# One-core mLSTM and feed-forward kernel: w_out's scale tile moved to the state products' bank, the first product's terms regrouped, the queues reordered

## Chip, cores and metric

One Trainium2 chip, one core. The metric is the device time of one execution in microseconds, as the median of several runs.

## What is computed

An mLSTM layer over B = 4, H = 8, S = 768, D = 40, written below as a loop over time, and behind it a feed-forward layer whose middle is h times softmax(h), normalised by rows. The output is 3072 x 320.

```python
m_new = maximum(f + m, i)
C = exp(f + m - m_new) * C + exp(i - m_new) * outer(v, k)
n = exp(f + m - m_new) * n + exp(i - m_new) * k
y = sigmoid(o) * (C @ q) / maximum(abs(n @ q), 1)
...
h = x @ w_in                                  # 320 -> 1024
solu = h * softmax(h)
ln = (solu - mean) / sqrt(var + 1e-6) * g_ln
out = ln @ w_out                              # 1024 -> 320
```

## The kernel before

The time loop is cut into six chunks of 128 steps. A unit is one chunk of one batch; there are 24 units, `u = 4 * c + b`, four for each chunk `c`, and units of one batch hand on the state `C`. What a unit does, in order of its data:

- Gates and scores. ScalarE (ACT) makes a 128 x 1024 decay tile `d` by exponentials (L1225 for the first four units, from a matmul spread L1158; L1214 for the others, from `gb`, which is loaded and masked by GpSimd (POOL, L1199)). TensorE (PE) makes scores (L1283, two banks of PSUM), VectorE (DVE) multiplies them with `d` to `p` (L1296).
- `y`. TensorE multiplies `q` with the state (L1323, units from 4 on) and `p` with `v` (L1350, two halves) into a third bank, VectorE scales and divides (L1336, L1365 to L1377), GpSimd multiplies with the sigmoid of the output gate (`x`, L1391; the sigmoids of eight units are taken at once, L1252). TensorE makes the state's increment (L1419).
- First product. `x` becomes two f16 tiles, a high and a low part (`xq`, ACT L1456 and POOL L1463, L1470), turned by a DMA transpose (L1484) to `xT`. TensorE multiplies `xT` with `w_in`, held as high (`wih`) and low (`wil`) f16 parts, into `ph`, 1024 columns: two half-depth matmuls (L1500) and then seven terms of two matmuls of 512 columns each (L1514), which are queued as three operations of two, two and three terms.
- Middle and second product. DVE and ACT make `us` from `ph` (L1530 to L1596), a DMA transpose turns it (`big<-us`, L1605), TensorE multiplies it with `w_out`'s high and low parts in four operations of six matmuls of 320 columns (L1660), ACT scales it to `ot` (L1677), which is stored.

The weights come as pairs of 32-bit words and are decoded, scaled and split on the chip in the first third of the run. For `w_in`: ACT L790 and DVE L800, L809 decode, ACT L858 sums magnitudes, the largest goes through TensorE (L880, L893) and DVE makes the scale `wsc` (L904); then ACT scales (L932) and casts the high part (L942, L955), POOL subtracts for the low part (L939), and small DMAs lay the last rows (L967). For `w_out`: L790, L800, L809, ACT L1005 sums, DVE L1023 to L1025 takes the largest and that of `g_ln` (`g`, L1684), TensorE transposes (L1028), DVE reduces (L1032), TensorE spreads (L1039), DVE makes `gs` and `ow` (L1046 to L1050), then ACT and DVE make the high and low parts (L1057, L1067).

The work of all units and of the set-up is a list of 1,314 numbered operations with reads and writes. Their order on every queue is a table, `ORDER`; each engine works its queue strictly in that order. A pair `(a, b)` in the table is a joint operation: the matmuls of two operations of TensorE are issued interleaved. A triple `(a, -1, n)` puts `n` filler matmuls (L1698, on the identity, results unused) ahead of operation `a`; operations in `BESIDE` get a small unused matmul after each step (L1702). Tiles are rings: a tile's first writer waits until the last user of the tile that had the buffer is done. Rings that matter here: `ph` has two PSUM tiles, `sy` three banks (scores, `y`), `so_` one bank (state increments and second products). `P.place` sets a tile's place in its ring's order; the small tile in which w_out's scale is made (`WOR`) stands in `ph` ahead of unit 0's product (place -0.4).

```python
for n in range(filled.get(n, 0)) ...          # fillers, in run()
steps = [((i + 0.5) / f.n, i, f) for f in (a, b) for i in range(f.n)]
for _, i, f in sorted(steps, key=lambda t: t[:2]):
    f.step(self, i)                           # a joint operation
```

Of the kernel before, what the change touches and what calls it, by code (L numbers as in the profile page):

```python
# [39 lines left out]
def gdv(P):  # L40
# [5 lines left out]
BESIDE = (235,)  # L46
WIR, WOR = ("sy", -0.5), ("ph", -0.4)
# [424 lines left out]
def mlstm_moe_kernel(ctx: ExitStack, tc: tile.TileContext, tok, qkT, og, fi0, fg, ig, w_in, w_out, gln, out):  # L472
# [646 lines left out]
    def unit(u):  # L1119
# [371 lines left out]
        ph = ("ph", u)  # L1491
# [4 lines left out]
        w_2 = [(*WIH, 4), (*WIL, 4), (*WIL, 5)]  # L1496
# [259 lines left out]
```

## Time and profile before

| what | us |
|---|---|
| median of 3 runs (283.72 to 286.01) | 283.91 |
| profiled execution: its own time | 283.8 |
| profiled execution: span, first to last instruction | 282.0 |
| PE busy in the span | 272.2 |
| ACT busy | 219.3 |
| DVE busy | 198.0 |
| POOL busy | 168.7 |

PE's busy time is that of its matmul records; where a matmul is issued while the one before still drains, the records overlap, so what TensorE is paid for an operation is read from the starts of successive rows and not from the durations. PEld are the loads of stationary operands, which overlap. DMA share is the mean busy share of the 16 DMA engines. All DMAs are issued from one queue (SP). Line numbers are those of the kernel before; in the changed kernel the same statements stand one or two lines lower.

### The profile page before, as it was taken

What the parts mean: (1) busy time and instruction counts of PE and PEld (TensorE: products, weight loads), DVE (VectorE), ACT (ScalarE), POOL (GpSimd) and SP (SyncE); (2) the same over time, 40 slices, a digit from 0 to 9 for tenths busy, and PEclk for the clock granted to TensorE, in tenths of its full rate; (3) what the DMA queues carried; (4) which work ended last, traced back from release to release, by engine and by line L of the source; (5) the groups of instructions that cost most, each with busy time, mean ns of one, the idle gap of its engine ahead of it and who ended that gap; (6) DMA issues with size and microseconds to landing.
All of it is one profiled execution on the core that took longest, in us unless ns stands there. A gap on an engine that the chain in (4) does not pass through costs nothing.

```text
span 282.0 us, 6383 instructions
## 1 busy us (share of the span) xinstructions
PE 272.2 (97%) x2253; PEld 214.1 (76%) x2253; DVE 198.0 (70%) x460; ACT 219.3 (78%) x473; POOL 168.7 (60%) x278
## 2 busy tenths in 40 slices
PE   6999999999997999999999999999999999999994
PEld 6977997877885787788787787888777886755673
DVE  3948885999977396776777968475887656656740
ACT  3778999999979778877749888898767749556851
POOL 5015999865864787584458764793757932653410
PEclk9999999999999999999999999999999999999999
DMA  6999989899999896799999999969799992457511
GB/s 210 369 397 364 283 184 256 236 219 246 264 304 218 220 235 149 167 226 247 166 275 217 301 198 313 196 152 197 244 213 263 217 236 54 92 108 160 88 50 46
DMA packets 85440, 60.49 MB, mean 215 GB/s; under 512 B 68016, under 2 KB 75312, under 8 KB 85408
## 3 DMA queue, kind: packets, MB, share of 16 engines
q1 hardware_dynamic: 85408, 60.08, 87.6%
q8 instruction: 18, 0.29, 0.4%
q14 instruction: 14, 0.11, 0.2%
HBM read 39.16 MB, written 4.26 MB: 154 GB/s over the span
## 4 chain that ended last, share of the span: by engine, by line
PE 75%; DMA 9%; POOL 4%; DVE 4%; issue 4%; ACT 2%; SPq 0%; POOLq 0%; ACTq 0%; DVEq 0%
PE ph L1514 19%; PE sy L1350 9%; PE sy L1283 6%; PE ph L1698 5%; DMA xT<-xq 5%; DMA big<-us 4%; PE sy L1323 4%; PE ph L1500 2%; PE so__1285 L1660 1%; PE so__2951 L1660 1%; PE so__3737 L1660 1%; PE ph L1158 1%; PE so__3793 L1660 1%; DVE nm L1530 1%; PE so__3093 L1660 1%
## 5 line engine op out<-in xcount | busy, mean ns | idle before, releaser
L1660 PEld LDWEIGHTS <-big 128*128 128x128 f16 x576 | 61.8, 113 | 20.1 <-DMA big<-us 2.7
L1350 PEld LDWEIGHTS sy<-tk,p 128*128 128x128 f32 x384 | 57.9, 192 | 4.7
L1514 PE MATMUL ph<-wih,xT 128*128 128x512 f16 x192 | 60.7, 381 | 0.0
L1350 PE MATMUL sy<-tk,p 128*128 128x41 f32 x384 | 55.6, 246 | 0.0
L1214 ACT ACTIVATE d<-gb,bG 128x128 f32<-128x128 f32 x160 | 50.6, 391 | 5.5 <-POOL kt L1265 2.8
L1514 PEld LDWEIGHTS <-xT 128*128 128x128 f16 x336 | 37.8, 118 | 17.8 <-issue 1.4
L1514 PE MATMUL ph<-wil,xT 128*128 128x512 f16 x144 | 48.8, 381 | 0.0
L1296 DVE TENSOR_TENSOR p<-sy,d 128x512 f32<-128x512 f32 x48 | 32.4, 683 | 8.6 <-PE sy L1283 8.1
L1589 ACT ACTIVATE us<-e,mu 128x1024 f16<-128x1024 f32 x24 | 27.3, 1143 | 9.8 <-DVE mu L1581 7.1
L1544 ACT ACTIVATE e<-ph,nh,hs 128x1024 f32<-128x1024 f32 x24 | 28.7, 1196 | 7.6 <-DVE nh L1537 5.4
L1596 DVE SCALAR_TENSOR_TENSOR us<-e,mu,us 128x1024 f16<-128x1024 f32 x24 | 31.7, 1320 | 2.8 <-ACT us L1589 2.6
L1530 DVE TENSOR_REDUCE nm<-ph 128x1 f32<-128x1024 f32 x24 | 29.2, 1217 | 5.9 <-PE ph L1514 5.8
L1553 DVE SCALAR_TENSOR_TENSOR e<-ph,e 128x1024 f32<-128x1024 f32 x24 | 29.2, 1215 | 5.9 <-ACT e L1544 5.8
L1643 POOL TENSOR_TENSOR pw<-ab,mhalf 128x1 f32<-128x1 f32 x24 | 16.6, 694 | 27.6 <-DVE ab L1637 21.6
L1199 POOL TENSOR_SCALAR_AFFINE_SELECT gb<-gb 128x1024 f32<-128x1024 f32 x20 | 23.4, 1170 | 12.0 <-DMA gb<-gd 12.0
L1323 PEld LDWEIGHTS sy<-C,qk 128*128 128x128 f32 x160 | 27.7, 190 | 3.4 <-PE sy L1283 0.5
L1463 POOL TENSOR_TENSOR xs<-x,xr 128x320 f32<-128x320 f32 x24 | 20.4, 850 | 15.9 <-DVE xr L1404 12.7
L1563 ACT ACTIVATE sq<-e,a 128x1024 bf16<-128x1024 f32 x24 | 27.4, 1140 | 0.8 <-DVE e L1553 0.7
L1391 POOL TENSOR_TENSOR x<-x,sg 128x320 f32<-128x320 f32 x24 | 21.9, 914 | 10.0 <-DVE x L1377 9.4
L1323 PE MATMUL sy<-C,qk 128*128 128x82 f32 x160 | 27.1, 257 | 0.4 <-DVE x L1377 0.4
L1283 PE MATMUL sy<-qk 64*128 64x128 f32 x384 | 26.6, 276 | 0.1
L1283 PEld LDWEIGHTS sy<-qk 64*128 64x128 f32 x384 | 24.9, 188 | 2.1 <-issue 1.1
(255 smaller groups left out, 565.4 us busy)
## 6 DMA issues: line engine op xcount, KB each, us to landing
gb<-gd SPq DMA_DIRECT2D x20, 512.0 KB, 5.2
qk<-in_qkT_dram SPq DMA_DIRECT2D x21, 448.0 KB, 5.3
tk<-in_tok_dram SPq DMA_DIRECT2D x24, 324.0 KB, 5.4
sg<-in_og_dram SPq DMA_DIRECT2D x12, 320.0 KB, 5.4
out_dram<-ot SPq DMA_DIRECT2D x24, 160.0 KB, 3.4
big<-in_w_in_dram SPq DMA_DIRECT2D x5, 512.0 KB, 6.6
big<-in_w_out_dram SPq DMA_DIRECT2D x4, 640.0 KB, 8.6
qk<-in_qkT_dram SPq DMA_DIRECT2D x3, 512.0 KB, 8.9
```

What stands on the lines that cost most here:

```text
L1214: nc.scalar.activation(out=P[d_t][:, j, n, :], in_=P[gb][:, h, :], func=AF.Exp, bias=P[BG][:, 0, c - 1, b * H + h : b * H + h + 1],)
L1283: nc.tensor.matmul(P[ps[j]][:, n * L : (n + 1) * L], lhsT=P[qk][r, 1, n, :], rhs=P[qk][r, 0, n, :], start=True, stop=True,)
L1296: lambda P, j=j: V.tensor_tensor(out=P[p_t][:, j], in0=P[ps[j]].rearrange("p (n l) -> p n l", l=L), in1=P[d_t][:, j], op=ALU.mult,),
L1323: nc.tensor.matmul(P[yk][:, n * 2 * E1 : (n + 1) * 2 * E1], lhsT=P[qk][:, 0, n, :], rhs=P[old][:, n, :], start=first_of_bank(), stop=False ...
L1350: nc.tensor.matmul(yv(P)[:, h, :], lhsT=P[p_t][:, j, n, :], rhs=v1(P)[:, h, :], start=first_of_bank(), stop=True, skip_group_check=True,)
L1514: nc.tensor.matmul(P[ph][:, j * 512 : (j + 1) * 512], lhsT=P[xT][:, a, :], rhs=P[w][:, k, j * 512 : (j + 1) * 512], start=False, stop=n == 6,)
L1530: lambda P: V.tensor_reduce(out=P[nm], in_=P[ph], axis=AX.X, op=ALU.max, negate=True),
L1544: lambda P: nc.scalar.activation(out=P[e], in_=P[ph], func=AF.Exp, bias=P[nh], scale=P[hs], accum_out=P[z]),
L1553: lambda P: V.scalar_tensor_tensor(out=P[e], in0=P[ph], scalar=2.0**-15, in1=P[e], op0=ALU.mult, op1=ALU.mult, accum_out=P[a]),
L1563: lambda P: nc.scalar.activation(out=P[sq], in_=P[e], func=AF.Square, bias=P[a], scale=-float(DFF), accum_out=P[su]),
L1596: lambda P: V.scalar_tensor_tensor(out=P[us][:, 1], in0=P[e], scalar=P[mu], in1=P[us][:, 0], op0=ALU.add, op1=ALU.subtract),
L1660: nc.tensor.matmul(P[po][:, 0:DM], lhsT=uTv(P, a)[:, k, :], rhs=P[w][:, k, :], start=n == 0, stop=n == 23)
```

## The change

Four edits: two constants (`BESIDE` and `WOR`), the order of the terms with the weights each operation waits for, and the whole table `ORDER`, of which the first lines are shown.

```diff
-BESIDE = (235,)
-WIR, WOR = ("sy", -0.5), ("ph", -0.4)
+BESIDE = (142, 281,)
+WIR, WOR = ("sy", -0.5), ("so_", 3.35)
...
 ORDER = [
-    18, 196, 19, 5, 37, 35, 3, 0, 17, 33, 34, 4, 1, 42, 289, 32, 47, 7, 127, 6, 31, 130, 8, 11, 52, 9, 10, 57, 12, 14,
...
+    0, 5, 33, 31, 18, 4, 19, 17, 37, 34, 3, 42, 1, 7, 47, 32, 127, 8, 11, 9, 52, 6, 150, 57, 243, 10, 289, 12, 20, 14,
...
-        terms = [(0, WIH, 0), (0, WIL, 0), (1, WIH, 1), (1, WIL, 1), (3, WIH, 0), (4, WIH, 1), (2, WIL, 2)]
-        w_k = [[(*w, 2 * k + j) for w in (WIH, WIL) for j in range(2)] for k in range(2)]
-        w_2 = [(*WIH, 4), (*WIL, 4), (*WIL, 5)]
+        terms = [(0, WIH, 0), (3, WIH, 0), (1, WIH, 1), (4, WIH, 1), (0, WIL, 0), (1, WIL, 1), (2, WIL, 2)]
+        w_h = [[(*WIH, 2 * k + j) for j in range(2)] for k in range(2)]
+        w_2 = [(*WIH, 4), (*WIL, 4)]
+        w_l = [(*WIL, n) for n in (0, 1, 2, 3, 5)]
...
-        for n0, n1, ws in ((0, 2, w_k[0]), (2, 4, w_k[1]), (4, 7, w_2)):
+        for n0, n1, ws in ((0, 2, w_h[0]), (2, 4, w_h[1]), (4, 7, w_l)):
```

In numbers over the whole table: fillers 65 before and 61 now (43 of them ahead of the gates' transposes L710 before, 36 now), joint operations 69 before and 63 now. From the first product on, 19 of 19 products with the state (L1323) were joint; now 15 of 20 are.

ACT's queue of the kernel before, from the scaling of w_in (`e<-e,wsc`) to the sigmoids (`sg`); `wt` decodes, `wih` is the cast of a high part, `wj,wm` a sum of w_out, `d<-ph` a decay tile:

```order
L942 CAST wih_342<-e_141 128x512
L932 ACTIVATE e_247<-e_247,wsc_333 128x512
L1225 ACTIVATE d_360<-ph_327 128x1024
L955 CAST w4_369<-e_247 128x512
L790 ACTIVATE wt_372<-big_175 128x640
L942 CAST wih_342<-e_170 128x512
L932 ACTIVATE e_170<-e_170,wsc_333 128x512
L1005 ACTIVATE wj_404,wm_403<-wg_274 128x640
L1225 ACTIVATE d_418<-ph_328 128x1024
L942 CAST wih_342<-e_170 128x512
L1252 ACT_TABLE_LOAD
L1252 ACTIVATE sg_117<-sg_117 128x2560
```

The same queue now:

```order
L791 ACTIVATE wt_332<-big_216 128x640
L956 CAST w4_335<-e_252 128x512
L933 ACTIVATE e_221<-e_221,wsc_303 128x512
L943 CAST wih_349<-e_141 128x512
L933 ACTIVATE e_221<-e_221,wsc_303 128x512
L943 CAST wih_349<-e_141 128x512
L1226 ACTIVATE d_380<-ph_314 128x1024
L943 CAST wih_349<-e_221 128x512
L791 ACTIVATE wt_397<-big_227 128x640
L1226 ACTIVATE d_408<-ph_320 128x1024
L1253 ACT_TABLE_LOAD
L1253 ACTIVATE sg_152<-sg_152 128x2560
```

One more scaling and one more decode of w_out (`wt_332`) stand ahead of the sigmoids, a sum of w_out (L1005) behind them, and what follows the sigmoids at once is now unit 0's L1401.

TensorE's queue of the kernel before, from unit 4's scores to the first product of unit 0 (`wmx` and `w` are w_out's scale):

```order
L1283 MATMUL sy<-qk_168 128x128 x8
L1323 MATMUL sy<-C_318,qk_168 128x82 x4
L1028 MATMUL ph<-ident,wmx 1x128
L1698 MATMUL ph<-ident 128x128 x2
L1039 MATMUL ph<-w_600,ones 128x1
L1500 LDWEIGHTS xT
L1500 MATMUL ph<-wih,xT 128x512
```

The same place now, and, behind the four matmuls of 512 columns shared with L1324 and four more, the place of w_out's scale:

```order
L1420 MATMUL so__544<-tk,kt_101 104x82 x4
L1284 MATMUL sy<-qk_239 128x128 x8
L1502 LDWEIGHTS xT
L1502 MATMUL ph<-wih,xT 128x512
L1502 LDWEIGHTS xT
L1502 MATMUL ph<-wil,xT 128x512
L1516 LDWEIGHTS xT
L1516 MATMUL ph<-wih,xT 128x512
L1324 MATMUL sy<-C_117,qk_239 128x82
```

```order
L1516 MATMUL ph<-wih,xT 128x512
L1516 LDWEIGHTS xT
L1516 MATMUL ph<-wih,xT 128x512
L1029 MATMUL so__616<-ident,wmx 1x128
L1516 LDWEIGHTS xT
L1516 MATMUL ph<-wil,xT 128x512
```

The product with the state moved from ahead of the first product into it, w_out's transpose from ahead of it to between its high and its low terms, and its tile from `ph` to `so_`.

SP's queue of the kernel before, from unit 4's `gb` to the first transpose (`g` is g_ln, `w4` w_in's last rows):

```order
L1172 DMA gb_367<-gd_180 128x1x1024
L1684 DMA g_389<-in_g_ln_dram 128x8x1
L1148 DMA qk1_168<-in_qkT_dram 112x1024
L967 DMA wih_342<-w4_369 64x512 x2
L967 DMA wil_407<-w4_369 64x512 x2
L1172 DMA gb_425<-gd_180 128x1x1024
L967 DMA wil_407<-w4_369 64x512 x2
L1484 DMA_TRANSPOSE xT_542<-xq_511 128x6x128
```

The same place now:

```order
L1149 DMA qk1_239<-in_qkT_dram 112x1024
L1173 DMA gb_479<-gd_361 128x1x1024
L968 DMA wih_349<-w4_335 64x512 x2
L968 DMA wil_382<-w4_335 64x512 x2
L1485 DMA_TRANSPOSE xT_518<-xq_494 128x6x128
L1686 DMA g_528<-in_g_ln_dram 128x8x1
L1145 DMA tk_533<-in_tok_dram 128x648
```

The load of `g`, six places ahead of the first transpose before, stands right behind it.

## Rows read from the trace of the kernel before

**Rows 1.** Busy time by stretch: length, PE, PEld, DVE, ACT, POOL, clock, DMA share, GB/s.

```profile
10.00:40.00 30.00, 29.85 (x276) 25.99 (x275) 22.81 (x55) 25.49 (x47) 15.93 (x20) 1.00 1.04 337
50.00:70.00 20.00, 19.63 (x159) 15.38 (x156) 19.63 (x44) 19.40 (x50) 13.57 (x20) 1.00 0.90 227
```

**Rows 2.** Waits of PE: total us, times, longest.

```profile
PE so__1285 L1660 <- DMA big<-us: 1.6, 1, 1.6
PE ph L1500 <- DMA xT<-xq: 0.8, 2, 0.6
```

**Rows 3.** Timeline of PE: start, us, operation, count, idle before and its releaser.

```profile
2.73 12.38 PE L1698 MATMUL ph<-ident 128*128 128x128 f32 x86 [2.73 <-POOL ident masks.py:199]
15.04 1.04 PE L710 MATMUL so__229<-ident,us 32*128 32x32 f32 x14
42.21 1.12 PE L1323 MATMUL sy<-C,qk 128*128 128x82 f32 x8
43.16 0.27 PE L1028 MATMUL ph<-ident,wmx 128*1 128x128 f32 x1
43.98 0.38 PE L1039 MATMUL ph<-w,ones 1*128 1x1 f32 x2
44.29 0.39 PE L1500 MATMUL ph<-wih,xT 64*128 64x512 f16 x1
```

**Rows 4.** Timeline of ACT.

```profile
16.18 0.29 ACT L722 COPY bG<-so__229 128x160 f32<-128x160 f32 x1 [1.80 <-PE so__229 L710]
23.49 1.34 ACT L932 ACTIVATE e<-e,wsc 128x512 f32<-128x512 f32 x2 [1.11 <-DVE wsc L904]
31.40 1.28 ACT L1252 ACT_TABLE_LOAD   x1
32.70 2.34 ACT L1252 ACTIVATE sg<-sg 128x2560 f32<-128x2560 f32 x1
```

**Rows 5.** Timeline of DVE, the gates' two long scans.

```profile
6.51 1.75 DVE L654 TENSOR_TENSOR_SCAN us<-p,us 32x768 f32<-32x768 f32 x1 [1.01 <-DMA p<-in_fg_dram]
10.91 1.47 DVE L678 TENSOR_TENSOR_SCAN us<-d,p 32x640 f32<-32x640 f32 x1
```

**Rows 6.** Groups of ACT by line and form, 0 to 60 us: busy, mean ns.

```profile
L932 ACT ACTIVATE e<-e,wsc 128x512 f32<-128x512 f32 x5 | 3.5, 721 | 1.1 <-DVE wsc L904 1.1
L790 ACT ACTIVATE wt<-big 128x640 f32<-128x640 f32 x4 | 3.2, 800 | 0.0
L1005 ACT ACTIVATE wj<-wg 128x640 bf16<-128x640 f32 x4 | 2.9, 730 | 0.0
```

**Rows 7.** Timeline of POOL.

```profile
35.11 1.69 POOL L1391 TENSOR_TENSOR x<-x,sg 128x320 f32<-128x320 f32 x2 [0.60 <-ACT sg L1252]
38.25 1.15 POOL L1470 TENSOR_TENSOR xq<-xs,xq 128x256 f16<-128x256 f32 x2
41.09 2.27 POOL L939 TENSOR_TENSOR wil<-e,wih 128x512 f16<-128x512 f32 x2
```

**Rows 8.** Timeline of SP, whose queue issues all DMAs.

```profile
39.42 1.31 SPq L1484 DMA_TRANSPOSE xT<-xq  x1
```

**Rows 9.** DMA issues, 25 to 43 us: count, KB each, median us to landing.

```profile
g<-in_g_ln_dram SPq DMA_DIRECT2D x1, 4.0 KB, 11.2
xT<-xq SPq DMA_TRANSPOSE x1, 3.0
```

**Rows 10.** Timeline of PE, first product of unit 3.

```profile
64.54 0.39 PE L1514 MATMUL ph<-wih,xT 128*128 128x512 f16 x1
66.14 0.59 PE L1514 MATMUL ph<-wih,xT 128*128 128x512 f16 x2
67.01 1.03 PE L1514 MATMUL ph<-wih,xT 128*128 128x512 f16 x4
```

**Rows 11.** Timeline of PE, its two longest waits behind 45 us.

```profile
57.94 0.42 PE L1323 MATMUL sy<-C,qk 128*128 128x82 f32 x2 [0.37 <-DVE x L1377]
...
90.48 0.31 PE L1660 MATMUL so__1285<-woh,big 128*128 128x320 f16 x1 [1.63 <-DMA big<-us]
```

123 rows, old and new, of the table ORDER are left out of this document.

## Prediction

> **What bounds the kernel now.** I read the waits of TensorE first, then the timelines of the queues in the first third, and last the busy time by stretch.
>
> The list of waits [rows 2] says that TensorE hardly ever waits: 1.6 us for one transpose of `us`, 0.8 for two transposes of `xT`, and a few tenths for others, one of them the 0.37 us at 57.94 [rows 11]. From the moment the first product starts, at 44.29 [rows 3], the run is thus a queue of TensorE's work with some 3 us of waits in it. What ends the run is when this queue starts, what stands in it, and those waits.
>
> Ahead of 44.29 TensorE looks just as busy [rows 1], but part of it is padding: 65 fillers stand there, 43 of them in the row of 12.38 us at 2.73 [rows 3]. What the first product waits for is read backwards. It is issued behind w_out's scale (L1039, 43.98) [rows 3]. Its input, unit 0's `xT`, was issued at 39.42 [rows 8] and landed 3.0 us later [rows 9], at 42.4. That waited for POOL's `xq` (38.25 + 1.15 = 39.40) [rows 7], a chain that begins with POOL's `x` at 35.11, which had waited for ACT's sigmoids [rows 7]. These ran from 32.70 to 35.04, behind a table load at 31.40 [rows 4]. ACT then had a full queue back to 23.49, where it had waited 1.11 us for w_in's scale, and before that 1.80 us for the gates' transposes [rows 4]. So the start of the first product is set by ACT's queue, and that by how early the gates and w_in's scale come. The DMA engines are full beside it (share 1.04 from 10 to 40 us) [rows 1], but the sigmoids' input is no longer late: its loads are moved ahead of the gates' stores.
>
> **The change part by part.**
>
> *Start of the first product.* Now the gates' first load and the load of `f` go out ahead of w_in's first block. DVE's first long scan waited 1.01 us for `f` and began at 6.51 [rows 5]; without that wait, and with the gates' small steps some 0.4 us earlier because their load is the first one issued, I put it at 5.1. The second scan ended at 10.91 + 1.47 = 12.38 [rows 5]; two decode steps that stood between them go behind, so about 9.9. The identity is POOL's first work now, so the fillers start at about 1.5 in place of 2.73; 36 of them take 36/43 x 12.38 = 10.4 us [rows 3], to about 12.0. The gates' transposes start there and not at 15.04, and are done 1.04 us later [rows 3], at 13.1. ACT's wait for them, which ended at 16.18 [rows 4], ends 3 us earlier; behind it stand w_in's decodes and sums, of which one had to follow the wait and three now do, so that about half of the 3 us is left at their end, 1.7. From there to the scale DVE and TensorE have less in between (the scale's last step is put ahead of the first `p`), which I count as 1.6 more. w_in's scale is then there at about 20.0, and ACT, which has two decay tiles to do first, begins its scalings at 20.2, not 23.49.
>
> From that row to the table load ACT needed 31.40 - 23.49 = 7.91 us [rows 4]. One scaling (0.72) and one decode (0.80) come in, one sum (0.73 and its read-out, about 0.9) goes out [rows 6]: +0.6. So the table load comes at 20.2 + 7.91 + 0.6 = 28.7 and the sigmoids end at 28.7 + (35.04 - 31.40) = 32.3, 2.7 earlier. From the start of `x` to the end of `xq` POOL took 39.40 - 35.11 = 4.3 us [rows 7]; with one low part (2.27 / 2 = 1.1) [rows 7] in between where another unit's `x` (1.69 / 2 = 0.85) and a product for `kt` stood, 3.8. The transpose is issued at 36.1 and lands at 39.1.
>
> TensorE itself gives nearly the same moment: from 15.04 to 42.21 [rows 3] it worked 27.2 us, in which 20 fillers stood; now 25 do, at 12.38/43 = 0.29 us at most +1.4, and waits of up to 1 us may go. 12.0 + 27.2 + 1.4 less those is 39.6 to 40.6. I take 40.1, that is 4.2 us early. The ends: 39.1, if TensorE does not hold it, and 42.2, if half of the lead is lost to the full DMA queue.
>
> That the first product can start there needs the regrouping: its last low weights came from POOL at 41.09 + 2.27 = 43.36 [rows 7]. The five high operations need none of the first four low blocks, and the low ones are due only some 3 us later. With the old grouping this start would be held to when POOL is through, 41 to 42.
>
> *Work that moved behind the start.* The product with unit 4's state (L1323) is now in the first product. Four terms with such a product took 66.14 - 64.54 = 1.60 us for two terms, two terms alone 67.01 - 66.14 = 0.87 [rows 10], so it costs 0.73 in company. w_out's scale costs 44.29 - 43.98 = 0.31 at its second matmul [rows 3], and a tenth at its first. Together +1.1.
>
> *Joint operations lost.* Five of the 20 products with the state now stand alone. Alone one takes 43.16 - 42.21 = 0.95 to the next operation's start [rows 3]; against 0.73 that is 5 x 0.22 = +1.1. One product with `v` and one state increment more stand alone: between nothing and as much each as those, +0.4 together.
>
> *Regrouped terms, the `beside` matmuls, w_out's tile in `so_`.* The 14 matmuls of a first product are the same, each with its own stationary load, so no cost. Four small matmuls more stand beside unit 0's `y`, in a stretch that has fillers anyway: between nothing and 0.3, taken as nothing. In `so_` the tile keeps the bank from unit 3's increment to unit 4's, and nothing is queued for that bank meanwhile; nothing.
>
> *Waits.* The wait at 90.48 (1.63) [rows 11] ends with a transpose of unit 2's `us`. In DVE's queue the last step of that `us` now stands ahead of two more steps of units 3 and 4 behind which it stood, so I take this wait as gone, and the 0.37 at 57.94 too, since unit 5's `x` has more room there: -2.0. Two thirds of the table are new, and unit 0's own `us` is made later than before (behind unit 1's exponentials and a `p`), with its second product due 3 us sooner. I take +1.2 for new waits; the bounds are nothing and 3.0, as much as the kernel before has in all.
>
> Sum: -4.2 + 1.1 + 1.1 + 0.4 - 2.0 + 1.2 = -2.4. The profiled execution took 283.8 us, 0.1 under the median shown, so 281.4 either way.
>
> **A rule against the change.** The load of `g` (L1684) now stands right behind the first transpose, and w_out's scale needs it, and TensorE has that scale between the high and the low terms of its first product. The row says 11.2 us from issue to landing for its 4 KB; a transpose in the same stretch took 3.0 [rows 9]. So most of the 11.2 is, I think, what was queued ahead of it: it went out behind w_out's last block, a `tk` and a `gb`. The Trainium skill ("DMA: Bandwidth & Descriptors", Rules for kernel authors) says that a strided last dimension is lowered to one descriptor per element, which would be 1,024 for `g`. By that page's table (Measured) an estimate at 10.5 ns a packet on 16 engines is 0.7 us, which changes nothing; the row, taken as it stands, makes the third rival.
>
> **Rivals.**
> - *Larger gain.* The lead holds and the new order has no waits to speak of: -4.2 + 2.6 - 3.0 = -4.6, 279.2. For it: TensorE waits so little already [rows 2]. Against: 300 operations of TensorE moved.
> - *The lead is given back.* From 50 to 70 us DVE is busy 19.63 and ACT 19.40 of 20 us [rows 1]. If these two set the pace there, starting TensorE early only makes it wait for `p` and `us` until 70, and the 1.5 us of lost pairs is paid as well: 283.8 + 1.5 - 1.6 (the wait at 90.48 still goes) = 283.7. Against: their early work starts earlier too.
> - *Slower: the scale of w_out stops TensorE.* `g` is issued at about 37.5. If it lands 11.2 later [rows 9], at 48.7, DVE's bound and TensorE's transpose follow at 49.3, in place of 42.8, and DVE, which works in order, holds unit 4's `y` behind it: 281.4 + 6.5 = 287.9. It costs from a landing at 42.2 on and makes the kernel slower than before from 44.7, that is 7.2 us after issue. For it: the row. Against: most of what was queued ahead of `g` then has landed by 39.
>
> **How the numbers follow.** The forecast case, 281.4 give or take 1.5, gets 0.52, nearly half of it below 281.1, which is 1% under the median (about what a measurement of this kernel can tell from no change). The larger gain gets 0.20, the lead given back 0.15, the slower case and other mishaps 0.13. So faster by over 1%: 0.25 + 0.20 = 0.45; within 1%: 0.27 + 0.15 = 0.42; slower: 0.13. The range goes from 278.3, a little under the larger gain, to 285.0, over the lead given back, and leaves out most of the slower case.
>
> **What would show it.** Right: the sigmoids end near 32.3, the first product starts near 40, `g` lands before 42, the first product's low terms follow its high ones without a gap at w_out's transpose (L1029 in the changed file), unit 2's second product starts without a wait, and TensorE's waits sum to 3 us or less. Wrong: a first product behind 42; a gap of TensorE at w_out's transpose; second products that wait for `big<-us` from unit 0 on; or single waits of TensorE on DVE spread over the last two thirds.

## The result and the profile after

The changed kernel took 280.19 us in the median of six runs (279.57 to 281.99), the kernel before 284.18 beside it (283.72 to 288.21): a ratio of 0.9864 with a 95% interval of 0.9817 to 0.9912. Timed a second time (`after_again` below) it came to 281.43 against 284.13, 0.9883 (0.9841 to 0.9925). The forecast was 281.4. The profiled execution took 281.67, with a span of 279.9; it is one of the longer ones, which matters further down. Medians are over all runs of a kernel; ratios leave out the runs more than 1.5% above its fastest, which show a lower granted clock.

Busy times of the page, to be held against the table of before: PE 0.8 us less, ACT 1.0 and POOL 2.8 less, DVE 1.7 more.

```profile
PE 271.4 (97%) x2249; PEld 213.0 (76%) x2249; DVE 199.7 (71%) x460; ACT 218.3 (78%) x473; POOL 165.9 (59%) x278
```

The set-up, which answers to [rows 3 to 8]. Timelines of DVE (the two long scans), ACT, POOL and SP:

```profile
5.07 1.74 DVE L655 TENSOR_TENSOR_SCAN us<-p,us 32x768 f32<-32x768 f32 x1
8.76 1.48 DVE L679 TENSOR_TENSOR_SCAN us<-d,p 32x640 f32<-32x640 f32 x1
```

```profile
12.67 0.30 ACT L717 ACTIVATE bG<-so__194 128x160 f32<-128x160 f32 x1 [0.53 <-PE so__194 L711]
19.56 1.95 ACT L933 ACTIVATE e<-e,wsc 128x512 f32<-128x512 f32 x3
29.25 1.28 ACT L1253 ACT_TABLE_LOAD   x1 [0.88 <-DMA sg<-in_og_dram]
30.54 2.34 ACT L1253 ACTIVATE sg<-sg 128x2560 f32<-128x2560 f32 x1
```

```profile
32.96 0.86 POOL L1392 TENSOR_TENSOR x<-x,sg 128x320 f32<-128x320 f32 x1 [1.66 <-ACT sg L1253]
35.70 0.94 POOL L1471 TENSOR_TENSOR xq<-xs,xq 128x256 f16<-128x256 f32 x2
41.79 1.16 POOL L940 TENSOR_TENSOR wil<-e,wih 128x512 f16<-128x512 f32 x1
```

```profile
36.66 1.33 SPq L1485 DMA_TRANSPOSE xT<-xq  x1
```

Each step is earlier than before by about what the forecast said: scalings 19.56 (23.49 before), table load 29.25 (31.40), transpose issued 36.66 (39.42). The transpose and `g`, DMA issues from 25 to 43 us (KB each, median us to landing), for [rows 9]:

```profile
xT<-xq SPq DMA_TRANSPOSE x1, 3.8
g<-in_g_ln_dram SPq DMA_DIRECT2D x1, 4.0 KB, 2.9
```

TensorE's timeline (first fillers, the gates' transposes, the first product, w_out's transpose, and every wait behind 45 us over 0.3 us), for [rows 3, 11]:

```profile
1.41 10.18 PE L1700 MATMUL ph<-ident 128*128 128x128 f32 x72 [1.41 <-POOL ident masks.py:199]
11.52 1.12 PE L711 MATMUL so__194<-ident,us 32*128 32x32 f32 x15
...
40.51 0.39 PE L1502 MATMUL ph<-wih,xT 64*128 64x512 f16 x1
...
43.30 0.27 PE L1029 MATMUL so__616<-ident,wmx 128*1 128x128 f32 x1
...
47.57 1.16 PE L1284 MATMUL sy<-qk 64*128 64x128 f32 x16 [0.57 <-DMA qk<-in_qkT_dram]
...
57.44 1.09 PE L1324 MATMUL sy<-C,qk 128*128 128x82 f32 x8 [0.79 <-DVE x L1378]
...
74.00 0.39 PE L1502 MATMUL ph<-wih,xT 64*128 64x512 f16 x1 [0.53 <-DVE rd L1369]
...
91.09 0.31 PE L1662 MATMUL so__1291<-woh,big 128*128 128x320 f16 x1 [1.37 <-DMA big<-us]
```

The first product starts at 40.51 and not at 44.29, 3.8 us early, right behind the landing of its `xT` (36.66 + 3.8 = 40.46). But TensorE now waits where it did not, and the wait for unit 2's `us` is still there (91.09, 90.48 before). Its list of waits, for [rows 2]:

```profile
PE so__1291 L1662 <- DMA big<-us: 1.4, 1, 1.4
PE sy L1324 <- DVE x L1378: 0.8, 1, 0.8
PE sy L1284 <- DMA qk<-in_qkT_dram: 0.6, 1, 0.6
PE ph L1502 <- DVE rd L1369: 0.5, 1, 0.5
```

and the two stretches of [rows 1]; from 50 to 70 us PE does less than before (19.21 busy, 19.63 before):

```profile
10.00:40.00 30.00, 29.82 (x279) 25.52 (x279) 24.05 (x59) 26.18 (x50) 17.06 (x19) 1.00 1.02 326
50.00:70.00 20.00, 19.21 (x160) 14.77 (x160) 18.22 (x39) 18.91 (x46) 14.41 (x23) 1.00 0.95 244
```

To see where the time is won, the two runs are compared at places by which TensorE has done exactly the same operations in both (fillers and the small matmuls of `BESIDE` aside, which all stand ahead of them): the starts of the first product (its half-depth matmul) of units 3, 5, 6 and 14. In us, read from the timelines of TensorE; the last column is the end of the last matmul, and the first (unit 0) shows the start only, since less work stands ahead of it now. The kernels below "changed" are the experiments, in which the same holds.

| kernel | unit 0 | unit 3 | unit 5 | unit 6 | unit 14 | last end |
|---|---|---|---|---|---|---|
| before | 44.29 | 63.33 | 83.03 | 95.08 | 170.51 | 278.46 |
| changed | 40.51 | 62.68 | 83.28 | 95.06 | 170.41 | 276.41 |
| after_again | 41.16 | 62.69 | 83.16 | 95.04 | 170.39 | 276.37 |
| hold_start | 42.15 | 62.88 | 82.95 | 94.61 | 169.96 | 276.17 |
| old_terms | 40.24 | 61.77 | 81.78 | 93.31 | 168.66 | 274.53 |
| old_wor | 42.31 | 62.94 | 82.95 | 94.64 | 169.99 | 276.26 |
| swap_qk | 40.64 | 62.23 | 82.78 | 93.10 | 168.93 | 274.80 |
| head_new | 40.89 | 61.69 | 81.70 | 93.20 | 174.50 | 281.08 |
| head_94 | 40.63 | 61.37 | 81.38 | 91.70 | 167.22 | 273.96 |
| swap_94 | 40.65 | 62.56 | 82.88 | 93.20 | 168.71 | 276.22 |
| head_40 | 43.87 | 66.39 | 86.09 | 97.81 | 172.76 | 279.58 |
| tail_40 | 43.57 | 65.97 | 86.09 | 97.95 | 173.30 | 279.16 |
| tail_new | 44.13 | 63.14 | 82.84 | 95.36 | 170.71 | 276.71 |
| tail_190 | 44.35 | 63.37 | 83.07 | 95.34 | 170.29 | 276.22 |

In the profiled execution the lead of 3.8 us is 0.65 at unit 3 and gone at unit 5 (83.28 against 83.03). The 2.05 us by which it ends earlier (276.41 against 278.46) are all won behind unit 14, where the forecast had counted nothing. So a number near the forecast could have been right for a wrong reason. That is what the runs had to tell.

### The profile page after: what moved, and what is told of

Read it like the earlier page. It is cut to its first block, busy times and chain, and to the rows that moved or that the text cites. A ratio compares the mean times of both kernels' runs of the same rounds, so it can differ in the third digit from the quotient of the medians.

```text
span 279.9 us, 6373 instructions
## 1 busy us (share of the span) xinstructions
PE 271.4 (97%) x2249; PEld 213.0 (76%) x2249; DVE 199.7 (71%) x460; ACT 218.3 (78%) x473; POOL 165.9 (59%) x278
## 4 chain that ended last, share of the span: by engine, by line
PE 67%; DMA 11%; DVE 11%; ACT 4%; issue 3%; POOL 2%; DVEq 0%; POOLq 0%; ACTq 0%
PE ph L1516 20%; PE sy L1351 6%; PE sy L1284 5%; PE sy L1324 4%; DMA sg<-in_og_dram 4%; DMA big<-us 3%; PE ph L1502 2%; DMA big<-in_w_out_dram 2%; DVE e L1555 2%; DVE p L1297 2%; DMA gd<-us 1%; DVE wol L1068 1%; DVE us L1598 1%; PE so__1291 L1662 1%; PE so__2649 L1662 1%
## 5 line engine op out<-in xcount | busy, mean ns | idle before, releaser
L1516 PE MATMUL ph<-wih,xT 128*128 128x512 f16 x192 | 58.9, 381 | 0.0
L1215 ACT ACTIVATE d<-gb,bG 128x128 f32<-128x128 f32 x160 | 50.0, 389 | 5.5 <-POOL kt L1266 4.2
L1516 PE MATMUL ph<-wil,xT 128*128 128x512 f16 x144 | 42.0, 380 | 0.0
L1297 DVE TENSOR_TENSOR p<-sy,d 128x512 f32<-128x512 f32 x48 | 32.3, 685 | 8.6 <-ACT d L1215 5.4
L1555 DVE SCALAR_TENSOR_TENSOR e<-ph,e 128x1024 f32<-128x1024 f32 x24 | 29.2, 1216 | 11.2 <-ACT e L1546 11.1
L1464 POOL TENSOR_TENSOR xs<-x,xr 128x320 f32<-128x320 f32 x24 | 18.2, 760 | 29.3 <-DVE xr L1405 23.4
L1546 ACT ACTIVATE e<-ph,nh,hs 128x1024 f32<-128x1024 f32 x24 | 28.7, 1195 | 7.2 <-DVE nh L1539 6.6
L1471 POOL TENSOR_TENSOR xq<-xs,xq 128x256 f16<-128x256 f32 (+1 forms) x48 | 24.6, 533 | 8.8 <-issue 7.1
L1324 PEld LDWEIGHTS sy<-C,qk 128*128 128x128 f32 x160 | 26.6, 191 | 3.9 <-PE sy L1284 1.0
L1392 POOL TENSOR_TENSOR x<-x,sg 128x320 f32<-128x320 f32 x24 | 20.7, 862 | 12.4 <-DVE x L1378 10.5
L1324 PE MATMUL sy<-C,qk 128*128 128x82 f32 x160 | 25.6, 259 | 0.8 <-DVE x L1378 0.8
L1200 POOL TENSOR_SCALAR_AFFINE_SELECT gb<-gb 128x1024 f32<-128x1024 f32 x20 | 22.5, 1127 | 2.6 <-DMA gb<-gd 2.4
```

Of the source, the lines that this page charges most:

```text
L1215: nc.scalar.activation(out=P[d_t][:, j, n, :], in_=P[gb][:, h, :], func=AF.Exp, bias=P[BG][:, 0, c - 1, b * H + h : b * H + h + 1],)
L1297: lambda P, j=j: V.tensor_tensor(out=P[p_t][:, j], in0=P[ps[j]].rearrange("p (n l) -> p n l", l=L), in1=P[d_t][:, j], op=ALU.mult,),
L1324: nc.tensor.matmul(P[yk][:, n * 2 * E1 : (n + 1) * 2 * E1], lhsT=P[qk][:, 0, n, :], rhs=P[old][:, n, :], start=first_of_bank(), stop=False ...
L1516: nc.tensor.matmul(P[ph][:, j * 512 : (j + 1) * 512], lhsT=P[xT][:, a, :], rhs=P[w][:, k, j * 512 : (j + 1) * 512], start=False, stop=n == 6,)
L1546: lambda P: nc.scalar.activation(out=P[e], in_=P[ph], func=AF.Exp, bias=P[nh], scale=P[hs], accum_out=P[z]),
L1555: lambda P: V.scalar_tensor_tensor(out=P[e], in0=P[ph], scalar=2.0**-15, in1=P[e], op0=ALU.mult, op1=ALU.mult, accum_out=P[a]),
```

## The experiments

Theory A is the forecast's: the early start is the gain. Theory B: the early start is lost by 91 us, and the gain comes from the order of the last third. Theory C, formed after the first four runs: both count. Kernels named `head_` follow the changed table up to some point and the old one behind it, `tail_` the other way round. The cuts are at places where the two tables have issued the same operations but for three to six, none of them TensorE's; the diffs show the seam.

| kernel | median us | before beside it | ratio, 95% interval |
|---|---|---|---|
| head_new | 287.88 | 284.74 | 1.0110 (1.0072 to 1.0148) |
| tail_new | 282.47 | 284.74 | 0.9931 (0.9897 to 0.9964) |
| hold_start | 281.53 | 284.74 | 0.9899 (0.9858 to 0.9939) |
| old_terms | 280.81 | 284.74 | 0.9858 (0.9813 to 0.9903) |
| head_94 | 281.00 | 284.13 | 0.9872 (0.9827 to 0.9918) |
| tail_190 | 282.08 | 284.13 | 0.9925 (0.9897 to 0.9953) |
| swap_qk | 280.40 | 284.13 | 0.9854 (0.9813 to 0.9894) |
| after_again | 281.43 | 284.13 | 0.9883 (0.9841 to 0.9925) |
| head_40 | 283.68 | 284.73 | 0.9953 (0.9913 to 0.9993) |
| tail_40 | 284.28 | 284.73 | 1.0001 (0.9964 to 1.0038) |
| swap_94 | 280.93 | 284.73 | 0.9837 (0.9777 to 0.9898) |
| old_wor | 280.74 | 284.73 | 0.9840 (0.9785 to 0.9894) |

The last two ratios look better than the medians beside them (280.93 and 280.74 to 284.73 are 0.987 and 0.986); with the widest intervals of the table they say no more than the others.

**head_new and tail_new: the table cut at the end of unit 2's second product.**

```diff
     304, 626, 269, 400,
-    494, 270, 446, 630,
+    628, 676, 674, 270,
...
```

> Queues of the changed kernel up to the end of unit 2's second product (about 94 us), the order of the kernel before from there to the end; the constants and terms are the changed ones. Theory A (the forecast's: the early start of the first product is the gain, the rest of the table is neutral): 280 to 281.5 us, as the changed kernel. Theory B (the lead is used up by about 91 us, because unit 2's transposed us lands no earlier, and the gain comes from the order behind 170 us): 283.5 to 285 us, no faster than the kernel before. Between the two, near 282, both parts count.

```diff
     (269, 586), 539, 492, 544,
-    270, 587, 446, 630,
+    493, 724, 437, 494,
...
```

> The complement: the kernel before with its own constants and terms up to the end of unit 2's second product (about 95 us), the changed order from there. Theory A: 283.5 to 285 us, no gain. Theory B: 280 to 282.3 us; the profiles differ by 2.0 us of work done by the end that was not there at 190 us, so 284.2 - 2.0 = 282.2 at least.

The tail alone gives 0.7% (0.4 to 1.0), some 2 us, as B and C say and A does not. The head alone came out slower, but for a reason of its own. The seam put one masking step of POOL (operation 676) ahead of unit 7's `xq`; its load had just been issued, and POOL, which works in order, stood still. POOL's and TensorE's timelines of `head_new`:

```profile
99.43 1.09 POOL L1200 TENSOR_SCALAR_AFFINE_SELECT gb<-gb 128x1024 f32<-128x1024 f32 x1 [7.33 <-DMA gb<-gd]
```

```profile
105.19 0.41 PE L1351 MATMUL sy<-tk,p 128*128 128x41 f32 x2 [4.43 <-DVE sy L1337]
```

Up to that seam its queues are the changed kernel's, and there it was 1.9 us ahead of before (unit 6 at 93.20 against 95.08). So the run tells nothing of the head's worth, except that the changed front can keep a lead that the profiled execution had lost.

**head_94: the same without that stall**, and **after_again: the changed kernel a second time.**

```diff
-    628, 676, 674, 270,
+    628, 674, 270,
...
-    450, 548, 549, 313,
+    450, 548, 549, 676, 313,
```

> As head_new (changed order to the end of unit 2's second product, order of before behind it), with one step of POOL moved back: the masking of unit 11's gb stands behind unit 8's xq again, as in the changed kernel, where head_new had it ahead of unit 7's xq and held POOL, and by that everything, for 7.3 us. The lead in work done at 96 us was 2.0 us in head_new before that stall. Theory C (front and tail count for about as much each): the lead stays, 284.4 - 2.0 = 282.4 us. Theory B (the front is worth nothing): 284 to 285 us. Theory A (the front is all): 280.5 us.

> The changed kernel once more, for a second profile beside the first, which took 1.5 us more than the median. Theory C: 280.2 us; TensorE's waits at 47.57, 57.44 and 74.00 (together 1.9 us) are not there in this execution, and it has done 1.5 to 2 us more work than the kernel before by 76 us. Theory B: they are there in each execution and the lead is gone by 76 us.

The front alone gives 1.3% (0.8 to 1.7), 3.1 us by the medians. B falls. So does A: the tail alone gave 2 us. C holds in kind, but the two do not add up: 3.1 and 2.0 would be 5.1, and the whole change gave 4.0 and 2.7 in its two timings. `after_again` says why a profile may show either. Its profile repeats the first one (unit 5 at 83.16, 281.55 us), against what C expected of it: the wait at 57.44 is there (0.80), the one at 74.00 too (TensorE's timeline of `after_again` puts it down to `xT`), only the one at 47.57 is not, and the lead is gone.

```profile
73.88 0.39 PE L1502 MATMUL ph<-wih,xT 64*128 64x512 f16 x1 [0.40 <-DMA xT<-xq]
```

`head_94` has the same queues up to 94 us and is 1.65 ahead at unit 5. TensorE's waits in it (the fillers' first one left out) are 0.5 us in all; the wait for unit 2's `us` near 90 us is not among them, and at unit 6 the lead is 3.4 us:

```profile
PE so__1370 L1420 <- ACT ot L1679: 0.3, 1, 0.3
PE ph L1502 <- DMA xT<-xq: 0.2, 1, 0.2
```

That `us` was issued at 80.72 and landed 6.3 us later, at 86.97, behind the same loads behind which it took 8.4 us in the changed kernel; why is open.

What parts these executions can be followed from 40 us on. One `gb` of 512 KB, issued at 40.2 to 40.5 in all of them, landed at 46.41 and 46.42 in the two profiles of the changed kernel and at 44.88 and 44.66 in `head_new` and `head_94`. Behind it stand POOL's mask and ACT's decay tile. Timelines of POOL and of ACT in the changed kernel:

```profile
46.47 1.09 POOL L1200 TENSOR_SCALAR_AFFINE_SELECT gb<-gb 128x1024 f32<-128x1024 f32 x1 [1.81 <-DMA gb<-gd]
```

```profile
47.60 1.28 ACT L1215 ACTIVATE d<-gb,bG 128x128 f32<-128x128 f32 x4 [1.25 <-POOL gb L1200]
```

and the same two steps in `head_94`:

```profile
44.72 1.09 POOL L1200 TENSOR_SCALAR_AFFINE_SELECT gb<-gb 128x1024 f32<-128x1024 f32 x1 [0.31 <-DMA gb<-gd]
```

```profile
46.00 1.26 ACT L1215 ACTIVATE d<-gb,bG 128x128 f32<-128x128 f32 x4
```

The decay is 1.6 us later in the one, and unit 5's product 1.9. In the four executions the order of the landings (44.66, 44.88, 46.41, 46.42) is that of unit 5's start to within 0.1 (81.38, 81.70, 83.28, 83.16).

The five other profiles with this order up to unit 5 fit. From the start of the first product to that of unit 5's, TensorE takes 40.6 to 40.8 us in `head_94`, `head_new` and `hold_start` (landing at 44.66 to 44.88) and in `old_wor` (45.93, but its first product starts only at 42.31), and 41.5 in `old_terms` (45.03), 0.65 of it a wait of its own. Where the landing comes at 45.96 to 46.42 and the start by 41.2 (`swap_qk`, `swap_94`, the changed kernel twice) it takes 42.0 to 42.8, and these four alone wait the 0.8 us near 57. That this landing is the cause is read from rows; a kernel that loads this `gb` earlier was not tried, and why the same queue lands it 1.7 us apart stays open.

**tail_190: only what lies behind unit 16's product.**

```diff
     1174, 811, (958, 948), 1089,
-    860, 1131, 908, (1091, 959),
+    908, (1091, 959), 950, 951,
...
```

> Kernel before up to unit 16's first product (about 193 us), changed order behind it only. If what the tail gives is won behind 193 us, as work done by time says: 282.5 us, as tail_new. If it is won between 95 and 193 us: 284 to 284.7 us.

As `tail_new`: the tail's gain is won behind 193 us. From unit 14's start to the last end the nine profiles with the new tail took 105.86 to 106.27 us, the five with the old one 106.58 (`head_new`) to 107.95 (before). So the old tail costs 0.3 to 2.1 us more, the most in the kernel before: part of the new tail's gain is had without it where the front is new, which is why the two don't add up. Single waits are part of it: unit 17's product in the kernel before (TensorE's timeline) and unit 19's in `swap_94` (0.78 us) wait longer than any wait behind unit 14 with the new tail (0.34).

```profile
197.89 0.39 PE L1500 MATMUL ph<-wih,xT 64*128 64x512 f16 x1 [0.57 <-DMA xT<-xq]
```

Without such waits some 0.9 us are left by the means; which rows of the table make them is open.

**hold_start, old_terms, old_wor: what the early start and the edits are worth.**

```diff
-    290, 321, 157, 291,
+    290, 321, (157, -1, 8), 291,
```

> The changed kernel with 8 more fillers ahead of unit 0's first product and nothing else: TensorE starts it some 2.2 us later (40.5 to about 42.7), the other engines' queues are untouched. Theory A: 2.2 us slower than the changed kernel, about 282.4 us. Theory B: the 2.2 us come out of a lead that is lost anyway: 280 to 280.7 us.

```diff
-        terms = [(0, WIH, 0), (3, WIH, 0), (1, WIH, 1), (4, WIH, 1), (0, WIL, 0), (1, WIL, 1), (2, WIL, 2)]
+        terms = [(0, WIH, 0), (0, WIL, 0), (1, WIH, 1), (1, WIL, 1), (3, WIH, 0), (4, WIH, 1), (2, WIL, 2)]
...
-        for n0, n1, ws in ((0, 2, w_h[0]), (2, 4, w_h[1]), (4, 7, w_l)):
+        for n0, n1, ws in ((0, 2, w_k[0]), (2, 4, w_k[1]), (4, 7, w_2)):
```

> The changed kernel with the terms in the old order and grouping (each high term followed by its low one, then the rest). Unit 0's product then needs the low block that POOL makes last, at 42.95 in the changed kernel's profile, at its third matmul (about 41.2), so TensorE stands still some 1.7 us there. Theory A: 1.7 us slower than the changed kernel, about 281.9 us. Theory B: 280 to 280.7 us.

```diff
-WIR, WOR = ("sy", -0.5), ("so_", 3.35)
+WIR, WOR = ("sy", -0.5), ("ph", -0.4)
...
-    290, 321, 157, 291,
+    290, 321, 106, 107, 157, 291,
...
```

> The changed kernel with w_out's scale tile back in ph's ring ahead of unit 0's product; for that its transpose, and the step of DVE that it waits for, stand ahead of the first product. The load of g lands at 40.9 and DVE needs 0.45 us, so the first product starts at about 41.5 and not 40.5. By what the 8 fillers cost (1.2 us for a start 2.2 later): 0.5 us slower than the changed kernel, 280.7 to 281.4 us; if the start does not matter here, as the changed kernel; a stop behind it, where unit 1's product needs the tile's bank, would show as a wait of TensorE near 48 us and cost more.

Unit 0's product starts 1.6 and 1.8 us later than in the changed kernel (42.15 and 42.31), and the ratios are 0.9899 and 0.9840, on either side of the changed kernel's 0.9864 and 0.9883. In the table both are 0.2 behind the changed kernel at unit 3 and ahead of it from unit 5 on. So in time the last 1.7 us of the lead buy nothing that can be told; `old_wor`'s stop near 48 us did not come. The rows say more where `gb` lands early: `hold_start` (44.85) is as late against `head_new` (44.88) at unit 5 as at the start, 1.25 and 1.26 us, and its last end is 1.6 us behind that of `old_terms` (45.03), which started 1.9 earlier. So the start is kept where this landing does not hold the next step, and worth nothing where it does, as in both profiles of the changed kernel. The old terms cost nothing that can be told either. TensorE's timeline of `old_terms` has the wait that the regrouping removes, and it is short, since the product's other matmuls and those with the state stand around it:

```profile
42.18 0.38 PE L1515 MATMUL ph<-wil,xT 128*128 128x512 f16 x1 [0.65 <-POOL wil L940]
```

**head_40 and tail_40: the table cut at the end of the set-up.**

```diff
     85, 100, 104, 370,
-    (288, -1, 1), 192, 369, 80,
+    2, 68, 192, 282,
...
```

> Changed order only for the set-up, up to the last y of unit 3 (about 38 us); behind it the order of before, in which w_out's scale and unit 4's product with the state stand ahead of the first product. The set-up ends 2 us earlier, the first product starts at 42 to 43 us. If what the front gives is the early set-up: 281.5 to 283 us. If it is the order from 40 to 94 us (first product ahead of w_out's scale, later loads): 283.7 to 285 us.

```diff
     244, 280, 104, 156,
-    192, 318, 282, 321,
+    318, (288, -1, 1), 192, 369,
...
```

> The complement: set-up in the order of before, from the last y of unit 3 on the changed order. The first product can start when its transpose lands, at about 42.4 us, 1.9 earlier than before, since w_out's scale stands behind it. If the early set-up is what counts: 282.2 us, as with the changed tail alone. If the order behind 40 us counts: 280.3 to 281.3 us, nearly as the changed kernel.

The early set-up alone gives 0.5% (0.1 to 0.9), about 1.3 us by the ratio; the new order behind 40 us on the old set-up gives nothing (1.0001), though the new tail is in it. The new order needs the new set-up: it asks for unit 0's `xT` before it has landed, and in the profiled execution the wait is paid twice. TensorE's timeline of `tail_40` and its busy time by stretch (columns as in [rows 1], the granted clock third from the end):

```profile
43.57 0.39 PE L1501 MATMUL ph<-wih,xT 64*128 64x512 f16 x1 [1.64 <-DMA xT<-xq]
```

```profile
43.00:44.00 1.00, 0.43 (x3) 0.20 (x4) 0.00 (x0) 1.00 (x5) 1.00 (x3) 1.00 0.83 292
44.00:45.00 1.00, 1.00 (x5) 0.82 (x5) 0.00 (x0) 0.95 (x4) 1.00 (x3) 0.51 1.05 345
45.00:46.00 1.00, 1.00 (x6) 0.91 (x5) 0.00 (x0) 0.56 (x2) 1.00 (x2) 0.50 1.21 147
46.00:47.00 1.00, 1.00 (x6) 0.91 (x6) 0.00 (x0) 0.00 (x0) 1.00 (x3) 0.50 0.82 38
47.00:48.00 1.00, 1.00 (x5) 0.38 (x4) 0.86 (x2) 0.00 (x0) 0.45 (x1) 0.79 1.06 310
```

Behind the idle 1.64 us the granted clock is 0.50, the lower of its two levels (1.2 GHz), until about 47.4. The two terms with the state's product took 3.00 us there, from 43.90 to 46.90, against 1.60 at the full clock [rows 10]. `head_40` has the same with unit 1's `xT` (1.78 us of wait, then 0.50 from 52 to 55 us), so both run 2.6 to 3.1 us behind the kernel before at unit 3.

The clock is not the whole of it. Seven of the twelve runs of `tail_40` had a mean granted clock of 0.999 or more (this profile 0.994); they take 283.48 us in the median, the kernel before 283.36 in its eight such runs, so the new tail's gain is missing there too. An estimate from the rows: the new order puts 1.7 us behind the start (`head_94`, up to unit 3), and on the old set-up the start is only 0.7 early (43.57), which leaves 1.0 us lost at the full clock, about what the new tail gives back.

**swap_qk and swap_94: the transpose that TensorE waits for near 90 us.**

```diff
-    350, 624, 306, 474, 262, 485, 222,
+    350, 306, 474, 262, 624, 485, 222,
```

> The changed kernel with one change of SP's queue: the load of unit 10's qk (448 KB) is issued behind the transpose of unit 2's us and not ahead of it. If TensorE's one long wait (1.1 to 1.4 us near 90 us for that transpose) comes from the DMA queue ahead of it, it goes and the time falls by 0.8 to 1.4 us, to about 279.2. If us itself is what comes late, or the time is taken back behind it: as the changed kernel, 280.2 us, within 0.4.

> Changed order up to 94 us with the load of unit 10's qk behind the transpose of unit 2's us, the order of before behind it. If the late transpose near 90 us costs time in most executions and the tail's order adds little to the front's: 279.5 to 280.3 us, the fastest. If not: as head_94, 281.0 us.

`swap_94` is `head_94` with this edit. The transpose of unit 2's `us`, issued at 82.61 in the changed kernel, landed at 91.05; with the 448 KB of `qk` behind it, it was issued at 81.50 and landed at 87.05. The wait is gone from the list of `swap_qk` (the fillers' first one left out):

```profile
PE ph L1502 <- DMA xT<-xq: 0.9, 2, 0.5
PE sy L1324 <- DVE x L1378: 0.8, 1, 0.8
```

`swap_94` has none there either. So the wait ends with the landing that the queue gives, as expected, though this order does not always make it: `head_94` lost it without the edit. In time it is a hint, no more: 280.40 against 281.43 for `after_again` on the same chip, with intervals that overlap. `swap_94` (280.93) is not faster than `head_94` (281.00), whose profile had no such wait to lose. None of these four kernels can be told from each other in time.

## Why the prediction was right, and where it was not

The number was right (281.4 forecast, 280.2 and 281.4 measured), the sum that gave it half.

- *Start of the first product, -4.2.* Measured -3.8 (40.51), and -3.1 to -3.7 in the other five profiles that have this set-up, these terms and this tile. The steps came where they were put: scan 5.1 and 5.07, scalings 20.2 and 19.56, table load 28.7 and 29.25, sigmoids done 32.3 and 32.9, first product 40.1 and 40.5. The transpose took 3.8 us and not 3.0, so `xT`, due at 39.1, landed at 40.46, just as TensorE came to it. One sentence was false. The sigmoids' input was said to be no longer late; the table load stood 0.88 us behind `sg`, the last load to land.
- *Work moved behind (+1.1), joint operations lost (+1.1 and +0.4).* By unit 3's product the lead shrinks from 3.7 to 2.0 in `head_94`, which has no wait on the way: 1.7 us, where 1.1 and part of the rest were due. Right in size as far as it can be read.
- *Waits that go, -2.0.* In the changed kernel this term failed. The wait at 90.48 is still there: 1.37 and 1.5 us in its two profiles, 1.1 to 1.3 in `old_terms`, `hold_start`, `old_wor` and `head_new`. The forecast looked at DVE's queue, where the last step of unit 2's `us` had come forward, and the transpose was indeed issued 1.2 us earlier (82.61 against 83.82). But it landed 0.6 us later, behind 448 KB of `qk`, with the DMA engines full (share 1.16 from 82.6 to 91 us). The wait at 57.94 did not go either (0.79 and 0.80, 0.37 before). In `head_94` both are gone, and its lead grows from 1.65 us at unit 5 to 3.38 at unit 6: there the term was paid as forecast.
- *New waits, +1.2, bounds nothing and 3.0.* Measured 0.57 + 0.79 + 0.53 = 1.9 in the first profile, of which the 0.79 takes the place of the 0.37; 0.5 in `head_94`, 0.2 of it at the start itself. Within the bounds, and it swings with the execution. All waits behind the start sum to 3.3 us in the first profile, over the 3 that the forecast had named.
- *The rest of the table, counted as nothing.* This is the gain that the sum did not have: 1.1 us behind unit 14 by the means of the nine and the five profiles (106.0 and 107.1), 1.95 between the two kernels' own profiles. It covers what the waits did not give, so the total came out right by luck.
- *The regrouping, said to be needed for the start.* With the old grouping the product started at 40.24 and then stood for 0.65 us, and the time was the same. The regrouping removes a real wait, which cannot be told in the times (280.81 us without it).
- *The lead is given back* (rival). That is what both profiles of the changed kernel show, though not by the cause named. DVE and ACT were less busy than before from 50 to 70 us (18.22 and 18.91 of 20); what came late was a landing. Over the six runs of `head_94` the front is worth about 1.3% without the new tail, so the rival falls for the time and holds for these executions.
- *The scale of w_out stops TensorE* (rival). `g` landed 2.9 us after issue, at 40.9, DVE's bound was done at 41.4, and at 43.30 TensorE takes the transpose without a gap. The 11.2 us of [rows 9] were mostly what was queued ahead of it, as argued: in the trace of before its packets of 4 bytes start from 33.0 us on, 6.7 after the issue at 26.33. The estimate of 0.7 us for them has a slip. The 10.5 ns of the Trainium skill ("DMA: Bandwidth & Descriptors", Measured) are 0.67 us divided by 64 packets, so dividing by 16 engines once more is not the page's; undivided, 1,024 packets would be an estimate of 10.8 us. The trace decides: 8.9 ns a packet on each engine in the mean, 0.6 us in all.

## What to carry to other kernels

An earlier start of the bounding engine is worth only what the next shared resource lets through: compare the two kernels at places where the engine has done the same work, and see where the lead goes. Where a wait ends with a DMA, look at what is queued ahead of that DMA and not only at when its input is made. One profile is one execution: a lead of 2 us came and went beside a single landing, so before a mechanism is believed, look at a second profile of the same queues.

## What the runs showed of the hardware

- A wait of TensorE of 1.64 us was followed by some 3.4 us at half the clock (`tail_40`), which cost 1.7 more: 1.40 on the two terms with the state's product, 0.27 on the next two (1.13, 0.86 at the full clock). The wait of 2.1 us near 90 us in `tail_new` was not: the granted clock stays at 1.00 from 85 to 95 us. What tells the two apart these runs do not show.
- The 4 KB of `g` go as 4-byte packets: 1,072 of that size start between 39.47 and 40.15 us in the trace of the changed kernel, 8.9 ns each in the mean, which is 0.6 us of 16 engines. In the DMA strip from 39.0 to 40.4 us (40 slices of 0.035 us, busy tenths and GB/s) most of them are the run of thirteen slices at 6 to 30 GB/s in which the engines are nearly full:

```profile
DMA  1114000299999999997799999999999209999990
GB/s 29 44 29 37 15 22 15 59 234 234 278 271 300 250 102 22 30 22 20 6 7 8 8 8 9 8 8 9 377 153 225 2 1 74 74 148 148 222 74 0
```

The Trainium skill ("DMA: Bandwidth & Descriptors", Rules for kernel authors) has one descriptor per element for a load with a strided last dimension, 1,024 here; by that rule, the trace agrees, with 1,072 packets, in which what else of that size moved then is counted too.
